# Second products with seven multiplications of eight: one fused DFT, gated MoE and MoE kernel on one core

## The chip, the cores and the metric

The kernel runs on one core of a Trainium2 chip. The metric is the device time of one execution in microseconds, the median of some runs. Every matmul in the main part is made in a 32-bit float format whose operands are rounded (F32R); to keep precision each operand is split in a high and a low part, and a product is three matmuls: high by high, high by low, low by high (`mm3`).

## The reference

```python
X = np.fft.fft(np.fft.fft(x, axis=1), axis=2).real           # x: (4, 3072, 256)
h = np.maximum(X @ w_in, 0.0)                                # (4, 3072, 1024)
u, v = h[..., :512], h[..., 512:]
v_n = (v - mean(v)) / np.sqrt(var(v) + 1e-06)
v_s = np.einsum('ts,bsd->btd', w_spatial, v_n) + b_spatial[None, :, None]
y = (u * v_s) @ w_out                                        # w_out: 512 x 256
x2 = y.reshape(12288, 256)
gate = 1.0 / (1.0 + np.exp(-(x2 @ w_gate)))                  # 256 x 1536
out = (gate * (x2 @ w_val)) @ moe2_w_out                     # 1536 x 256
```

## The kernel before

The kernel has three parts. The first (to about 254 us) makes the transform, U and V, and stores both to DRAM. The second (254 to 1751 us), which the change touches, multiplies by w_spatial and then by w_out. The third (to the end) is the last MoE.

In the second part the product with w_spatial is done in two halves p of the batch, each by seven products of blocks instead of eight (Strassen's scheme). `leaves` lists them: (p, i, c), where i is one of the seven products in the order 3, 5, 1, 7, 4, 2, 6, and c one of three columns of 512 tokens. A leaf multiplies a V operand (3072/2 rows by 512) by a W operand (3072/2 by 512 tokens) into four PSUM banks, one for each 128 rows d of 512. The loop over leaves is divided in sixths, kp = 0 to 5. In each sixth TensorE does 2 x 4 products of three matmuls, each of 128x128 weights by 512 columns: 24 in a sixth, 144 in a leaf. Leaves take turns between banks 0 to 3 and 4 to 7.

The order of the instructions on each engine is the order of the program. In each sixth the loop writes, in this order:

- `evacuate(before, ..., kp, ...)` in the first four sixths: VectorE adds bank d of the leaf before to the sums in `C` (and so frees the bank). Where i is in `FINAL` (5, 4, 2 and 6), the sum is one block of v_s. It is multiplied by max(U, 0) to g (`scalar_tensor_tensor`), ScalarE casts g to its high part `gh`, and the low part `gl` is left for `finish_gate`, which the next sixth calls.
- `advance`: it loads operands two sixths ahead of their preparation (SP's queue) and prepares those that are needed three sixths later (LEAD). ScalarE scales V (`norm_job`), VectorE adds or subtracts two blocks where the scheme wants it (L929 for V, L933 for W), ScalarE casts to the high part (L942), and VectorE makes the low part (L950) one job later. W operands have a ring of four buffers, V operands one of seven, loads one of seven staging tiles. V operands for the next i are made in the leaves with c = 2, one in each sixth.
- `side_loads` in the fifth sixth: bias and the first two blocks of U, from SP's queue. `load_u` for the other two blocks stands behind the use of the first two, since U has two buffers.
- the 24 matmuls of the sixth.
- `second`, behind the fifth and the sixth sixth, where the leaf before is in `FINAL`: one half o of 128 output columns, 4 x 3 matmuls of 512 columns against `wo`, a copy of the bank by ScalarE, and with o = 1 the store of the 128x2x512 block to `x2_d` from ScalarE's queue.
- `background` in other leaves: the weights of the last MoE and w_out are made from 64-bit words, a step at a time; GpSimd makes sums of blocks for the third part.

There are 24 leaves in `FINAL`, and so 24 second products. The last two are woven into the end of this part and the beginning of the third.

Of the kernel before, what the change touches and what calls it, by code (L numbers as in the profile page):

```python
# [10 lines left out]
F32 = mybir.dt.float32  # L11
# [12 lines left out]
DM = 256  # L24
FF2 = 1536
P = 128
# [134 lines left out]
def layouts(x, moe_w_in, moe_w_spatial, moe_b_spatial, moe_w_out, moe2_w_gate, moe2_w_val, moe2_w_out):  # L161
# [18 lines left out]
    for at in (0, 32, 64):  # L180
# [6 lines left out]
    wg, wv = (w.reshape(2, P, 12, P) for w in (moe2_w_gate, moe2_w_val))  # L187
    arrays = {
# [6 lines left out]
        "w_out": moe_w_out.reshape(4, P, DM).transpose(1, 0, 2).reshape(P, 2, 512),  # L195
# [44 lines left out]
def tile_kernel(ctx: ExitStack, tc: tile.TileContext, t: dict, out: bass.AP):  # L240
# [5 lines left out]
    wg_d = [dram.tile([P, 896], F32, name=f"wg_d{i}") for i in range(12)]  # L246
    wv_d = [dram.tile([P, 1024], F32, name=f"wv_d{i}") for i in range(3)]
# [920 lines left out]
    wo = [gp.tile([P, 2, 512], F32R, tag=f"wo{n}", name=f"wo{n}") for n in "hl"]  # L1168
# [3 lines left out]
    taken, begun, stores = [], [], []  # L1172

    def background():
# [5 lines left out]
        elif begun:  # L1180
            first, kind, i = begun.pop()
            value, = from64_rest(first, new())
            if kind == "second":
                split(wo[0][:, i, :], wo[1][:, i, :], value)
            elif kind == "out":
                stores.append((wv_d[i // 2][:, i % 2 * 512 : i % 2 * 512 + 512], value))
            else:
# [11 lines left out]
                stores.append((wg_d[i][:, 0:384], value[:, 0:384]))  # L1199
                stores.append((wg_d[i][:, 384:896], sums))  # L1200
        else:
            for to, value in stores:
                nc.sync.dma_start(to, value)
            stores.clear()
# [6 lines left out]
    def evacuate(leaf, ps, d, side):  # L1211
# [41 lines left out]
    def finish_gate(side):  # L1253
        if "low" in side:
            side.pop("low")()

    def load_u(side, d):
        u = gp.tile([P, 512], F32, tag="u", name="u", bufs=2)
        nc.sync.dma_start(u, side["u_of"][:, d, :])
        side["u"].append(u)  # L1260

    def side_loads(leaf, side):
        p, i, c = leaf
        if i in (3, 4, 5):
            at = ((3 if i == 3 else 0) + c) * 512
            side["bias"] = gp.tile([P, 512], F32, tag="bias", name="bias")
            nc.sync.dma_start(side["bias"], t["bt"][:, at : at + 512].to_broadcast([P, 512]))
# [8 lines left out]
    def second(leaf, o, bank, side):  # L1276
# [355 lines left out]
```

## Time and profile before

| | |
|---|---|
| median of 3 runs | 2842.23 us (2842.18 to 2842.6) |
| the profiled execution | 2841.18 us, span 2839.1 us |
| TensorE, VectorE, ScalarE busy | 2827.8, 1998.9, 1416.4 us |
| GpSimd busy | 235.5 us |
| granted TensorE clock | 1.00 |

The span is from the first to the last instruction of the program; some 2 us of the execution lie outside it. A row of a group of instructions gives their number, busy time and mean duration. Instructions of one engine are pipelined, so that the next can start before one has ended; durations then add up to more than the busy time, and what an instruction costs its engine is the distance from start to start. A matmul of 512 columns lasts 0.39 us in the trace, while the next starts 0.23 us after it.

### The profile page before, as it was taken

How to read it: one execution, taken by the hardware profiler on the slowest of the kernel's cores; microseconds unless marked ns; L12 is line 12 of the kernel's file. 1: busy time of each engine (PE TensorE's matmuls, PEld its weight loads, DVE VectorE, ACT ScalarE, POOL GpSimd, SP SyncE). 2: the span in 40 equal slices, each digit the busy share in tenths (PEclk: the TensorE clock that was granted, in tenths of full speed). 3: DMA queues.
4: the chain of work that ended last, by engine and by line, in shares of the span. 5: the costliest groups of instructions: out<-in, count | busy, mean ns of one | idle time of the engine just before them, and what ended most of it. 6: DMA issues, size and time to landing. Idle time of an engine off the chain costs nothing.

```text
span 2839.1 us, 34286 instructions
## 1 busy us (share of the span) xinstructions
PE 2827.8 (100%) x12630; PEld 2360.2 (83%) x12630; DVE 1998.9 (70%) x2936; ACT 1416.4 (50%) x2264; POOL 235.5 (8%) x348
## 2 busy tenths in 40 slices
PE   9999999999999999999999999999999999999999
PEld 7998888888888888888888888888888888888887
DVE  8877757778847666677756666876667666766665
ACT  6886434334424424433424424665655565656565
POOL 5984000011000000000000000000000000000000
PEclk9999999999999999999999999999999999999999
DMA  8888757778847766677866683100000000000000
GB/s 300 292 314 324 274 198 260 266 261 299 275 143 261 257 227 238 213 268 262 284 207 213 214 285 108 61 23 30 30 30 1 30 30 30 23 8 30 30 15 15
DMA packets 150953, 470.89 MB, mean 166 GB/s; under 512 B 16769, under 2 KB 18689, under 8 KB 150401
## 3 DMA queue, kind: packets, MB, share of 16 engines
q1 hardware_dynamic: 144448, 440.52, 45.0%
q0 software_dynamic: 2448, 14.82, 1.4%
q10 hardware_dynamic: 3888, 13.37, 1.2%
q8 instruction: 98, 1.61, 0.2%
q14 instruction: 71, 0.57, 0.1%
HBM read 386.07 MB, written 82.58 MB: 165 GB/s over the span
## 4 chain that ended last, share of the span: by engine, by line
PE 96%; DVE 2%; DMA 1%; ACT 1%; issue 0%; SPq 0%; ACTq 0%; DVEq 0%
PE bank L261 30%; PE bank L262 30%; PE bank L263 30%; PE psv L262 1%; PE psv L263 1%; PE psv L261 1%; PE psu L261 1%; PE psu L262 1%; PE psu L263 1%; PE psf L261 1%; PE psf L262 1%; PE psf L263 1%; DMA st<-v_d 1%; PE psv L730 0%; PE psu L768 0%
## 5 line engine op out<-in xcount | busy, mean ns | idle before, releaser
L262 PE MATMUL bank<-wl,vh 128*128 128x512 f32 x2016 | 784.4, 389 | 0.2 <-DVE wl L950 0.2
L261 PE MATMUL bank<-wh,vh 128*128 128x512 f32 x2016 | 784.3, 389 | 0.0
L263 PE MATMUL bank<-wh,vl 128*128 128x512 f32 x2016 | 784.2, 389 | 0.0
L942 ACT CAST wh<-st 128x1024 fp32r<-128x1024 f32 x249 | 260.9, 1049 | 382.9 <-PE bank L263 231.0
L262 PEld LDWEIGHTS bank<-wl,vh 128*128 128x128 f32 x2016 | 378.4, 188 | 79.5 <-DVE wl L950 0.8
L261 PEld LDWEIGHTS bank<-wh,vh 128*128 128x128 f32 x2016 | 378.4, 188 | 78.5
L263 PEld LDWEIGHTS bank<-wh,vl 128*128 128x128 f32 x2016 | 378.4, 188 | 78.3
L950 DVE TENSOR_TENSOR wl<-st,wh 128x1024 fp32r<-128x1024 f32 x249 | 306.8, 1233 | 169.4 <-ACT wh L942 168.9
L261 PE MATMUL bank<-x,wgh 128*128 128x512 f32 x673 | 262.4, 390 | 0.5 <-ACT t L1511 0.4
L1497 DVE TENSOR_TENSOR t<-t,bank 128x512 f32<-128x512 f32 x144 | 98.9, 687 | 231.4 <-PE bank L263 231.4
L262 PE MATMUL bank<-x,wgh 128*128 128x512 f32 x673 | 261.8, 389 | 0.0
L263 PE MATMUL bank<-x,wgl 128*128 128x512 f32 x673 | 261.8, 389 | 0.0
L933 DVE TENSOR_TENSOR st<-st 128x1024 f32<-128x1024 f32 x177 | 217.7, 1230 | 50.5 <-DMA st<-in_wt 50.5
L1520 DVE TENSOR_TENSOR gl<-s,gh 128x512 fp32r<-128x512 f32 x288 | 199.4, 692 | 57.8 <-ACT gh L1518 44.4
L262 PE MATMUL bank<-gl,wv 128*128 128x512 f32 x576 | 224.1, 389 | 0.0
L261 PE MATMUL bank<-gh,wv 128*128 128x512 f32 x576 | 224.1, 389 | 0.0
L263 PE MATMUL bank<-gh,wv 128*128 128x512 f32 x576 | 224.1, 389 | 0.0
L916 ACT ACTIVATE st<-st,ln_all 128x512 f32<-128x512 f32 x162 | 123.3, 809 | 140.5 <-DMA st<-v_d 115.7
L1485 ACT ACTIVATE s<-s 128x512 f32<-128x512 f32 x144 | 91.0, 632 | 153.8 <-DVE s L1484 153.7
L261 PEld LDWEIGHTS bank<-x,wgh 128*128 128x128 f32 x673 | 126.3, 188 | 28.5 <-ACT s L1482 0.9
L263 PEld LDWEIGHTS bank<-x,wgl 128*128 128x128 f32 x673 | 126.3, 188 | 26.3
L262 PEld LDWEIGHTS bank<-x,wgh 128*128 128x128 f32 x673 | 126.3, 188 | 26.0
(267 smaller groups left out, 4490.4 us busy)
## 6 DMA issues: line engine op xcount, KB each, us to landing
st<-in_wt SPq DMA_DIRECT2D x424, 512.0 KB, 5.5
st<-v_d SPq DMA_DIRECT2D x140, 512.0 KB, 4.7
u_d<-tu SPq DMA_DIRECT2D x64, 384.0 KB, 5.4
u<-u_d SPq DMA_DIRECT2D x96, 256.0 KB, 5.7
v_d<-tv SPq DMA_DIRECT2D x92, 256.0 KB, 5.1
x_d<-x ACTq DMA_DIRECT2D x24, 512.0 KB, 4.9
raw<-x_d SPq DMA_DIRECT2D x24, 512.0 KB, 7.1
xt<-in_xh SPq DMA_DIRECT2D x23, 512.0 KB, 5.2
```

What stands on the lines that cost most here:

```text
L261: nc.tensor.matmul(out=ps, lhsT=w[0], rhs=x[0], start=first, stop=False, **kw)
L262: nc.tensor.matmul(out=ps, lhsT=w[0], rhs=x[1], start=False, stop=False, **kw)
L263: nc.tensor.matmul(out=ps, lhsT=w[1], rhs=x[0], start=False, stop=last, **kw)
L916: nc.scalar.activation(st[:, k, :], st[:, k, :], AF.Identity, scale=scale[:, at], bias=shift[:, at])
L933: nc.vector.tensor_tensor(out=tiles[0], in0=tiles[0], in1=tiles[1], op=op)
L942: nc.scalar.copy(hl[0], st)
L950: eng.tensor_tensor(out=hl[1], in0=st, in1=f(hl[0]), op=ALU.subtract)
L1485: nc.scalar.activation(s1, s1, AF.Sigmoid)
L1497: nc.vector.tensor_tensor(out=g["t2"], in0=g["t2"], in1=g["b"], op=ALU.add)
L1520: nc.vector.tensor_tensor(out=l, in0=s, in1=f(h), op=ALU.subtract)
```

## The change

22 of the 24 second products (all but the last two) get a scheme with seven products of eight as well. The 512 tokens are taken in two halves of 256 (`HC`), and for each pair of 128-row blocks d the product of a 2x2 arrangement (two outputs o, two blocks d, two halves of columns) is made of seven terms:

- `evacuate` keeps g of an even d, and with the odd d VectorE makes four differences of 256 columns (two tiles `ta`, `tb`). `take_piece` casts the pieces: 256 columns of the first g, all 512 of the second, both tiles. Low parts follow in `finish_gate`; the last piece (`late`) is cast in the fifth sixth. Pieces have one buffer each.
- `second` does terms, each of three matmuls of 256 columns, into four banks (those that the leaf before used): six terms of the first pair behind the third sixth, the seventh behind the fourth, all seven of the second pair behind the fifth.
- `combine` adds up the four banks: one copy by ScalarE and six additions by VectorE, written behind `advance` of the last sixth. `send` stores both halves from ScalarE's queue.
- The weights are laid out in blocks a11, a12, a22, a21 as the third part has them, and `background` adds the sums s1 to s4 and splits them; a21 goes to DRAM (`wa_d`) for the last two products.
- U and bias are asked for on GpSimd's queue instead of SP's. `load_u` now stands ahead of the casts. Stores left over from `background` are sent at the start of a leaf.
- The last two second products keep 24 matmuls of 512 columns, in another order for the last but one (`plain`: the first pair for both halves behind the first block of the last leaf). Pieces and `wo` lie in a pool `mp` of their own, which is closed behind the last second product and opened anew for the third part.

```diff
-        if "parts" in side:
-            gh, gl = (x[at] for x in side["parts"])
-        else:
-            gh = gp.tile([P, 512], F32R, tag="gh", name="gh", bufs=4)
-            gl = gp.tile([P, 512], F32R, tag="gl", name="gl", bufs=4)
-        nc.scalar.copy(gh, g)
-        finish_gate(side)
-        side["low"] = lambda: nc.vector.tensor_tensor(out=gl, in0=g, in1=f(gh), op=ALU.subtract)
-        side["g"].append((gh, gl))
         if d < 2:
             load_u(side, d + 2)
+        finish_gate(side)
+        if leaf not in SEVEN:
+            if "parts" in side or d < 3:
+                take_piece(side, "g", d, g)
+            else:
+                side["late"] = lambda: take_piece(side, "g", d, g)
+            return
+        if d % 2 == 0:
+            side["raw"] = g
+            if d == 0:
+                take_piece(side, 0, 0, g[:, 0:HC])
+            return
+        b1, b2 = side.pop("raw"), g
+        if d == 1:
+            take_piece(side, 0, 1, b2)
+        else:
+            take_piece(side, 1, 0, b1[:, 0:HC])
+            side["late"] = lambda: take_piece(side, 1, 1, b2)
+        ta, tb = (gp.tile([P, 512], F32, tag="cv", name="t", bufs=4) for _ in range(2))
+        for to, x, y in (
+            (ta[:, 0:HC], b1[:, HC:], b1[:, 0:HC]),
+            (tb[:, 0:HC], b2[:, HC:], b1[:, HC:]),
+            (ta[:, HC:], b2[:, HC:], ta[:, 0:HC]),
+            (tb[:, HC:], b2[:, 0:HC], ta[:, HC:]),
+        ):
+            tt(out=to, in0=x, in1=y, op=ALU.subtract)
+        take_piece(side, d // 2, 2, ta)
+        take_piece(side, d // 2, 3, tb)
+
+    HC = 256
+
+    def take_piece(side, pair, i, src):
+        n = src.shape[-1]
+        if "parts" in side:
+            hi, lo = (x[:, i, :] for x in side["parts"])
+        else:
+            k = (2, 1, 3, 2)[i] if pair == "g" else i
+            hi, lo = (mp.tile([P, n], F32R, tag=f"{x}{k}", name=f"b{x}") for x in "hl")
+        nc.scalar.copy(hi, src)
+        side["g"][pair, i] = (hi, lo)
+        side["lows"].append(lambda: nc.vector.tensor_tensor(out=lo, in0=src, in1=f(hi), op=ALU.subtract))
 
     def finish_gate(side):
-        if "low" in side:
-            side.pop("low")()
+        while side["lows"]:
+            side["lows"].pop(0)()
+
...
     def load_u(side, d):
         u = gp.tile([P, 512], F32, tag="u", name="u", bufs=2)
-        nc.sync.dma_start(u, side["u_of"][:, d, :])
+        nc.gpsimd.dma_start(u, side["u_of"][:, d, :])
         side["u"].append(u)
...
+    TERMS = {
+        1: ("a11", 0, 0, 0, 0),
+        6: ("s2", 2, 1, 0, 1),
+        5: ("s1", 2, 0, 1, 0),
+        7: ("s3", 3, 0, 1, 1),
+        3: ("s4", 1, 1, 2, 0),
+        4: ("a22", 3, 1, 2, 1),
+        2: ("a12", 1, 0, 3, 0),
+    }
+
+    SEVEN = {leaf for leaf in leaves[:-2] if leaf[1] in FINAL}
...
+    def second(side, pair, terms, bank):
+
+        for term in terms:
+            w, piece, half, acc, at = TERMS[term]
+            first = acc not in side["acc"]
+            if first:
+                side["acc"][acc] = banks(bank + acc)
+            w = slice(W_AT[w] * P, W_AT[w] * P + P)
+            mm3(
+                side["acc"][acc][:, at * HC : at * HC + HC],
+                [x[:, pair, w] for x in wo],
+                [x[:, half * HC : half * HC + HC] for x in side["g"][pair, piece]],
+                first,
+                pair == 1,
+                skip_group_check=True,
+            )
+
+    def combine(side, part, both, to):
+
+        x, y, z, w = (side["acc"][k] for k in range(4))
+        tt = nc.vector.tensor_tensor
+        p1, u2 = part[:, 0:HC], part[:, HC:]
+        nc.scalar.copy(p1, x[:, 0:HC])
+        tt(out=u2, in0=p1, in1=x[:, HC:], op=ALU.add)
+        tt(
+            out=both.rearrange("p (k n) -> p k n", k=2),
+            in0=u2.unsqueeze(1).to_broadcast([P, 2, HC]),
+            in1=y.rearrange("p (k n) -> p k n", k=2),
+            op=ALU.add,
+        )
+        tt(out=to[1][:, HC:], in0=both[:, HC:], in1=y[:, 0:HC], op=ALU.add)
+        tt(out=to[0][:, HC:], in0=both[:, 0:HC], in1=z[:, 0:HC], op=ALU.add)
+        tt(out=to[1][:, 0:HC], in0=both[:, HC:], in1=z[:, HC:], op=ALU.add)
+        tt(out=to[0][:, 0:HC], in0=p1, in1=w[:, 0:HC], op=ALU.add)
+        side["to"] = to
+
+    def combine_cv(side):
+        combine(side, *(lambda a: (a[0], a[1], a[2:]))([gp.tile([P, 512], F32, tag="cv", name="y", bufs=4) for _ in range(4)]))
+
+    def send(leaf, side):
         p, i, c = leaf
         mem, th = FINAL[i]
-        finish_gate(side)
-        ps = banks(bank)
-        for d in range(4):
-            at = (d % 2) * 256 + o * P
-            mm3(ps, [w[:, d // 2, at : at + P] for w in wo], side["g"][d], d == 0, d == 3)
-        if o == 0:
-            side["x2"] = gp.tile([P, 2, 512], F32, tag="x2", name="x2", bufs=1)
-        nc.scalar.copy(side["x2"][:, o, :], ps)
-        if o == 1:
-            nc.scalar.dma_start(x2_d[(2 * p + mem) * 6 + 3 * th + c], side["x2"])
+        for o in range(2):
+            nc.scalar.dma_start(x2_d[(2 * p + mem) * 6 + 3 * th + c][:, o, :], side["to"][o])
...
+        side = new_side()
+        final = before is not None and before[0][1] in FINAL
+        seven = before is not None and before[0] in SEVEN
         for kp in range(6):
-            if before is not None:
-                if kp < 4:
-                    evacuate(before[0], before[1][kp], kp, before[2])
-                else:
-                    finish_gate(before[2])
+            if kp == 0 and final:
+                send_stores()
+            if before is not None and kp < 4:
+                evacuate(before[0], before[1][kp], kp, before[2])
+            if final and kp == 4:
+                before[2].pop("late")()
+                finish_gate(before[2])
             advance(6 * n + kp + LEAD, 2)
+            if seven and kp == 5:
+                combine_cv(before[2])
             if kp == 4:
                 side_loads(leaf, side)
             wh, wl = ready["w", (p, i, c, kp)]
...
                         kp == 0 and k == 0,
                         kp == 5 and k == 1,
                     )
-            if before is not None:
-                if kp >= 4 and before[0][1] in FINAL:
-                    second(before[0], kp - 4, 4 - base + kp - 2, before[2])
+            if seven and kp in (2, 3, 4):
+                second(before[2], kp // 4, ((1, 6, 5, 7, 4, 3), (2,), (1, 6, 5, 7, 4, 3, 2))[kp - 2], 4 - base)
+            if final and kp == 5:
+                send(before[0], before[2])
```

## Rows read from the trace of the kernel before

**Rows 1.** The page's busy table: busy us (share of the span) xinstructions
```profile
PE 2827.8 (100%) x12630; PEld 2360.2 (83%) x12630; DVE 1998.9 (70%) x2936; ACT 1416.4 (50%) x2264; POOL 235.5 (8%) x348
```

**Rows 2.** The page's chain that ended last, shares of the span by engine
```profile
PE 96%; DVE 2%; DMA 1%; ACT 1%; issue 0%; SPq 0%; ACTq 0%; DVEq 0%
```

**Rows 3.** Windows: length, busy us of PE, PEld, DVE, ACT, POOL, clock, DMA share, GB/s
```profile
422.80:460.88 38.08, 38.08 (x170) 31.53 (x169) 31.63 (x38) 22.79 (x28) 0.00 (x0) 1.00 0.82 275
...
1173.51:1211.59 38.08, 38.08 (x169) 31.53 (x168) 30.23 (x37) 22.16 (x28) 0.00 (x0) 1.00 0.78 259
...
694.79:732.88 38.09, 38.09 (x170) 31.53 (x169) 30.77 (x39) 10.88 (x14) 2.21 (x4) 1.00 0.74 251
...
809.03:847.12 38.09, 38.09 (x170) 31.53 (x169) 16.91 (x23) 10.89 (x14) 0.00 (x0) 1.00 0.53 176
```

**Rows 4.** Timeline of TensorE, 512 columns, first and last of 55: start us, us, what
```profile
799.74 0.39 PE L262 MATMUL bank<-gl,woh 128*128 128x512 f32 x1
...
811.98 0.39 PE L262 MATMUL bank<-wl,vh 128*128 128x512 f32 x1
```

**Rows 5.** Timeline of TensorE, 384 columns, first and last of 19
```profile
119.81 0.33 PE L261 MATMUL psf<-c,fh 128*128 128x384 f32 x1
...
122.95 0.33 PE L263 MATMUL psf<-c,fl 128*128 128x384 f32 x1
```

**Rows 6.** Timeline of TensorE at 12 us, full 32-bit matmuls, eight merged
```profile
11.82 1.89 PE L503 MATMUL psx<-xt,ln_all 128*128 128x256 f32 x8
```

**Rows 7.** Timeline of weight loads behind a wait
```profile
40.80 0.19 PEld L261 LDWEIGHTS psv<-gh,ph 128*128 128x128 f32 x1 [0.36 <-ACT ph L453]
40.91 0.19 PEld L262 LDWEIGHTS psv<-gl,ph 128*128 128x128 f32 x1
```

**Rows 8.** Timeline of VectorE before and in the stretch at 422.80
```profile
418.24 0.69 DVE L1223 TENSOR_TENSOR g<-c,bank 128x512 f32<-128x512 f32 x1 [9.12 <-PE bank L263]
...
426.74 0.68 DVE L1223 TENSOR_TENSOR g<-c,bank 128x512 f32<-128x512 f32 x1
427.34 0.68 DVE L1224 TENSOR_TENSOR c<-bias,bank 128x512 f32<-128x512 f32 x1
...
430.28 1.41 DVE L929 SCALAR_TENSOR_TENSOR st<-st,ln_all 128x512 f32<-128x512 f32 x2
431.68 1.22 DVE L950 TENSOR_TENSOR wl<-st,wh 128x1024 fp32r<-128x1024 f32 x1
...
441.29 1.22 DVE L933 TENSOR_TENSOR st<-st 128x1024 f32<-128x1024 f32 x1
442.43 1.22 DVE L950 TENSOR_TENSOR vl<-st,vh 128x1024 fp32r<-128x1024 f32 x1
```

**Rows 9.** Timeline of TensorE: second half of a second product, next leaf's first matmul
```profile
420.07 0.39 PE L261 MATMUL bank<-gh,woh 128*128 128x512 f32 x1
...
422.80 0.39 PE L261 MATMUL bank<-wh,vh 128*128 128x512 f32 x1
```

**Rows 10.** Groups of VectorE instructions by shape: xcount | busy us, mean ns | idle before
```profile
L528 DVE TENSOR_TENSOR words<-et 128x256 f32<-128x256 f32 x2 | 0.8, 417 | 0.0
```

**Rows 11.** Waits from 422.80 to 460.88: us in total, times, longest
```profile
ACT st L916 <- DMA st<-v_d: 5.2, 2, 2.6
...
DVE st L929 <- ACT st L916: 2.9, 2, 2.4
```

**Rows 12.** Waits of SP's queue in the same stretch
```profile
SPq L882 <- DVE wl L950: 13.7, 6, 4.8
```

**Rows 13.** DMA issues by tile: xcount, KB each, median us to landing
```profile
u<-u_d SPq DMA_DIRECT2D x96, 256.0 KB, 5.7
...
st<-in_wt POOLq DMA_DIRECT2D x8, 512.0 KB, 7.9
```

More of the change, by code (lines that the diff above doesn't have):

```diff
@@ L1172, in tile_kernel, with send_stores @@
     taken, begun, stores = [], [], []
+    def send_stores():
+        for to, value in stores:
+            nc.sync.dma_start(to, value)
+        stores.clear()
     def background():
@@ L1182, in background @@
             value, = from64_rest(first, new())
-            if kind == "second":
-                split(wo[0][:, i, :], wo[1][:, i, :], value)
-            elif kind == "out":
+            if kind == "out":
                 stores.append((wv_d[i // 2][:, i % 2 * 512 : i % 2 * 512 + 512], value))
@@ L1198, in background @@
                     nc.gpsimd.tensor_tensor(out=s, in0=x, in1=y, op=op)
[L1199 to L1204 removed]
+                if kind == "second":
+                    for at, src in ((slice(0, 384), value[:, 0:384]), (slice(384, 896), sums)):
+                        split(wo[0][:, i, at], wo[1][:, i, at], src)
+                    parts = gp.tile([P, 512], F32R, tag="cv", name="parts", bufs=4)
+                    split(parts[:, 0:P], parts[:, P : 2 * P], value[:, 384:512])
+                    stores.append((wa_d[:, i * 256 : i * 256 + 256], f(parts[:, 0:256])))
+                else:
+                    stores.append((wg_d[i][:, 0:384], value[:, 0:384]))
+                    stores.append((wg_d[i][:, 384:896], sums))
+        else:
+            send_stores()
             if todo64:
@@ L1274, in side_loads, with plain @@
                 load_u(side, d)
-    def second(leaf, o, bank, side):
+    TERMS = {
[8 more added lines that the diff above has]
+    SEVEN = {leaf for leaf in leaves[:-2] if leaf[1] in FINAL}
+    def plain(side, pair, o, bank):
+        if pair == 0:
+            side["acc"][o] = banks(bank)
+        for d in (2 * pair, 2 * pair + 1):
+            if (o, d % 2) == (1, 0):
+                w = [a21[:, pair * 256 + k * P : pair * 256 + k * P + P] for k in range(2)]
+            else:
+                at = W_AT[f"a{o + 1}{d % 2 + 1}"] * P
+                w = [x[:, pair, at : at + P] for x in wo]
+            mm3(side["acc"][o], w, side["g"]["g", d], d == 0, d == 3)
@@ new lines, in plain_out @@
+    def plain_out(side, o, to=None):
+        to = gp.tile([P, 512], F32, tag="cv", name="y", bufs=4) if to is None else to
+        nc.scalar.copy(to, side["acc"][o])
+        side.setdefault("to", []).append(to)
+    def second(side, pair, terms, bank):
[13 more added lines that the diff above has]
+            )
@@ L1446, in tile_kernel @@
         if d == 0:
+            for o in range(2):
+                plain(before[2], 0, o, 4 - base + 2 + o)
+            before[2].pop("late")()
+            finish_gate(before[2])
             split_wg(0, staged_b[0])
@@ L1451, in tile_kernel @@
         if d == 1:
-            second(before[0], 0, 4 - base + 2, before[2])
+            plain(before[2], 1, 0, None)
+            plain_out(before[2], 0)
             split_wg(1, staged_b[2])
@@ L1460, in tile_kernel @@
         if d == 2:
-            second(before[0], 1, 4 - base + 3, before[2])
+            plain(before[2], 1, 1, None)
+            plain_out(before[2], 1)
+            send(before[0], before[2])
             for step in steps[2:6]:
                 step()
-    before = (leaf, ps, side)
     wst = A["w"].tile([P, 1024], F32, tag="wl", name="wst")
@@ L1578, in tile_kernel @@
             steps[7]()
-            second(leaf, 0, base, side)
-            second(leaf, 1, base + 1, side)
+            for o in range(2):
+                for pair in range(2):
+                    plain(side, pair, o, base + o)
+            mix.close()
+            mp = pool(ra, "mp", 1, "right")
+            last_x2 = mp.tile([P, 2, 512], F32, tag="x2", name="x2", bufs=1)
+            for o in range(2):
+                plain_out(side, o, last_x2[:, o, :])
+            send(leaf, side)
             for k in range(2):
```

31 lines of the change are left out of this document (20 added, 11 removed).

## Prediction, written before the changed kernel ran

> **What bounds the kernel now.** I read the page's busy table first. TensorE is busy for 2827.8 of 2839.1 us, VectorE for 1998.9, ScalarE for 1416.4 [rows 1]; the chain that ended last is TensorE for 96% [rows 2]. So time can only come from fewer TensorE cycles, and only while nothing else becomes late. The change touches 22 leaves, so I looked at their stretches next [rows 3]. A stretch runs from the first matmul of a leaf to the first of the next and holds the second product of the leaf before. Each is 38.08 us, and TensorE is busy for all 38.08, granted clock 1.00 (2.4 GHz): there is no wait in them to win. Beside that VectorE differs: 31.63 us in the stretch at 422.80, where the next V operands are made as well, 16.91 in the one at 809.03, 30.77 in the one at 694.79, which still works off what the stretch before it left. Three products go with each V (L261 to L263), so 144 matmuls belong to the leaf and 24 to the second product.
>
> **TensorE, part by part.** Matmuls of 512 columns start 12.24 us / 54 = 0.2267 us apart [rows 4], those of 384 columns 3.14 / 18 = 0.1744 [rows 5]. The old second product is 24 x 0.2267 = 5.44 us. The new one is 2 pairs x 7 terms x 3 = 42 matmuls of 256 columns, a shape that this trace has only in another number format. By the line through the two rows 256 columns take 0.1744 - 0.0523 = 0.122 us. [...] I take 0.122, as a load that starts with the matmul before it is 0.11 ahead and so is hidden. 42 x 0.122 = 5.12 us: 0.32 saved, x 22 = **7.0 us less** (bounds: 18.0 less, 41 more). One product of eight saves little, because halving the columns takes 0.227 only to 0.122. The new stretch without waits is 32.64 + 5.12 = 37.76 us.
>
> **VectorE, per leaf.** Its instructions start closer than they last: 512 columns 0.60 us apart (426.74, 427.34), 1024 columns 1.14 (441.29, 442.43), a V sum of two 1.40 (430.28, 431.68) [rows 8]. For 256 columns the trace shows 417 ns of duration [rows 10]; 0.60 less the difference in duration (0.683 - 0.417) gives 0.334 apart. Added: eight differences, 8 x 0.334 = 2.67; low parts of eight pieces, 6 x 0.60 + 2 x 0.334 = 4.27 in place of 4 x 0.60; the sums of accumulators, 5 x 0.334 + 0.60 = 2.27. Together 6.8 us more. In the stretch at 809.03 that is 23.7 of 37.76 and costs nothing; at 694.79 it is 37.6, just covered, where work can still be late by up to 1 us. At 422.80 it is 38.4: more than the stretch has.
>
> There are six such stretches, those of the third column of leaves 5, 4 and 2 in both halves (31.63 and 30.23 us stand for them in rows 3). I made a ledger of one. VectorE can begin when the last leaf's first accumulator is done. Now that is at 418.24, 4.56 us ahead of the stretch, because the second half of the second product still follows on TensorE; the leaf's own matmuls end at 420.07 [rows 8, 9]. With all products moved ahead of the last sixth nothing follows, and the lead shrinks to 420.07 - 418.24 = 1.83. VectorE must come through to the third sum of accumulators, since the next leaf's second accumulator is the bank which that sum frees; it is needed three matmuls, 0.68 us, into the next stretch. So it has 1.83 + 37.76 + 0.68 = 40.27 us. Its work till then: evacuation 4 x 3 x 0.60 = 7.20; low parts 4.27; differences 2.67; V 6 x (1.40 + 1.14) = 15.24; W six low parts and three sums, 9 x 1.14 = 10.26; first three sums 0.33 + 0.60 + 0.42 = 1.35. Sum 40.99: overdrawn by 0.7 us if it never waits.
>
> It does wait. In this stretch it now idles 6.2 us, 3.0 of them because it is ahead; that part goes. The other part is that a V sum stands behind ScalarE's scaling (2.9 us), itself behind the V load (5.2) [rows 11], which SP issues when a staging tile comes free, 13.7 us of waiting for VectorE's low parts [rows 12]: a later VectorE asks later. New is that the scaling stands behind casts of pieces that wait for the differences. I take 2.0 us of such waits, between 0 and 4. So each of the six stretches ends 2.7 us late (0.7 to 4.7): **6 x 2.7 = 16 us more** (4 to 28). The next stretch has slack enough to begin afresh.
>
> **The rest, at nothing.** ScalarE gets four more casts, two of them short, and one short copy for two long ones, some 1.3 us a leaf, where it is busy 22.8 of 38.1 at most [rows 3]. Its casts for the second pair wait for TensorE's first products, as the pieces have one buffer each; behind them stands the cast of a W operand that TensorE takes two sixths (10.9 us) later; if that cover went, TensorE would wait by as much as the cast is late. The two stores on ScalarE's queue wait for the last sum; behind them stand the next leaf's first casts, which are made after VectorE's evacuation anyway. U and bias go from SP's queue to GpSimd's. GpSimd is idle in the six stretches and busy for at most 2.21 us in the others [rows 3]; a load that it issued landed after a median 7.9 us against 5.7 for U by SP [rows 13], and U is used two sixths after it is asked for. On SP the operand loads no longer stand behind U, which may bring them forward a little; I count nothing. The split of moe_w_out into 14 blocks lies in stretches without second products. The last two leaves keep 24 matmuls of 512 columns; the copies of the last one wait for both halves (0 to 1 us).
>
> **Sum.** 2841.18 us is the time of the profiled execution (span 2839.1 and 2.1 around it); - 7.0 + 16.2 gives 2850.4. The median of the runs is 1.05 above that execution: **2851.4 us**. The forecast's own range, with 1.7 to 3.7 us per stretch, is 2845 to 2857; the ends of the bounds, 0.7 and 4.7, give 2839 and 2863.
>
> **Rivals.**
> VectorE keeps up (faster). Place: the third sum of accumulators in the six stretches. It decides from the point where work and waits to that sum stay under 40.3 us; then only the 7.0 us remain: 2835. For it: my 256-column spacing is worked out, not seen, and 15 such instructions at 0.28 would close the overdraft. Against it: every wait must vanish as well. Chance 0.14.
>
> Short matmuls at their floor. At 0.11 us, the distance of two loads, TensorE saves 0.82 x 22 = 18 us; the stretch shrinks to 37.26, and the overdraft grows by 0.5 to 3.2: 19 us in six. 2841.2: no change. Against it: both rows of this format lie 13 to 14 ns above columns / 2.4. Chance 0.15. The Trainium skill (TensorE: Matmul & The Clock Gate, "Back-to-back issue gap") puts a warm start-to-start distance at columns / 2.4 plus about 2.5 ns, an estimate of 109 ns here; at 512 columns it gives 216 where rows 4 have 227, so in this number format the trace does not agree.
>
> The V loads are late too, since staging tiles come free later: 4.7 us per stretch or more, 28 - 7 = 21 us more, 2863. For it: that wait is in rows 11 already. Chance 0.18.
>
> Weight loads bind the short matmuls, at the 384-column distance. 42 x 0.1744 = 7.32 us, 1.88 more per leaf, 41 us more; the longer stretch (39.96) gives VectorE time, some 3 us of waits remain: 2886. Against it: two loads 0.11 apart. Chance 0.06.
>
> **How the numbers follow.** Forecast 0.47, rivals 0.14, 0.15, 0.18, 0.06. The range reaches from the kept pace to beyond the late loads: 2834 to 2870; the load-bound case and tails stay out. A measurement here tells 0.2% (5.7 us) from no change. Faster by more than that: most of the first rival and a tail of the second, 0.17. Within: the rest of these and the forecast's low end, 0.27. Slower: 0.56.
>
> **What would show it.** Right: 42 matmuls of 256 columns about 0.122 us apart; stretches of 37.7 to 37.8 us in some 16 of the 22; six of 39 to 42, each ending with TensorE waiting for a sum of accumulators on VectorE, VectorE busy from edge to edge there. Wrong: all 22 alike (VectorE keeps up); starts 0.11 or 0.17 apart; waits in the middle of stretches, at the terms behind the third or fifth sixth; or GpSimd's loads named as what ended VectorE's waits.

## The result and the profile after

The changed kernel takes **2883.03 us** (2881.78 to 2885.18, 4 runs) against 2842.41 (2842.18 to 2842.88) for the kernel before: ratio 1.0143, 95% interval 1.0128 to 1.0158. It is slower, as forecast, but by 40.6 us where 9 were expected; the range ended at 2870. The profiled run took 2884.23 us, span 2882.5.

The busy table and the chain that ended last, in place of [rows 1, 2]:

```profile
PE 2837.2 (98%) x13026; PEld 2380.7 (83%) x13026; DVE 2156.4 (75%) x3336; ACT 1440.4 (50%) x2334; POOL 302.1 (10%) x471
...
PE 74%; DVE 11%; DMA 8%; ACT 3%; issue 3%; SPq 0%; POOL 0%; ACTq 0%; DVEq 0%; POOLq 0%
...
PE bank L263 23%; PE bank L264 22%; PE bank L265 22%; DMA st<-v_d 5%; DVE wl L952 2%; DVE st L935 2%; DMA st<-in_wt 1%; DMA words<-in_w_b 1%; ACT st L918 1%; DVE vl L952 1%; ACT wh L944 1%; DVE st L931 1%; PE psv L264 1%; PE psv L265 1%; PE psv L263 1%
```

TensorE had 96% of the chain and has 74%. VectorE has 11%, and the loads of V (st<-v_d) have 5%: two engines and a queue now pass the end on to each other. TensorE's busy time has even grown by 9.4 us, though its columns are fewer; what that is comes below.

Windows of the changed kernel (length, busy us of PE, PEld, DVE, ACT, POOL, clock, DMA share, GB/s), in place of [rows 3]: two of the six overdrawn stretches, one without V operands, and the stretches behind the first two.

```profile
423.68:464.71 41.03, 37.90 (x187) 31.87 (x185) 38.63 (x54) 23.48 (x31) 2.71 (x5) 1.00 0.80 262
464.71:504.84 40.13, 39.76 (x187) 33.25 (x187) 34.50 (x54) 10.95 (x15) 1.09 (x2) 0.96 0.66 223
825.38:863.12 37.74, 37.74 (x187) 32.06 (x186) 24.19 (x43) 12.13 (x17) 2.19 (x4) 1.00 0.40 125
...
1194.93:1239.33 44.40, 37.90 (x187) 31.88 (x186) 38.62 (x54) 23.36 (x31) 2.72 (x5) 0.98 0.75 251
1239.33:1279.78 40.45, 40.45 (x187) 33.85 (x188) 34.51 (x54) 10.94 (x15) 2.72 (x5) 0.93 0.71 243
```

The undisturbed stretch is 37.74 us (37.76 forecast). The overdrawn ones are 41.03 and 44.40, with VectorE busy for 38.6, and the stretches behind them are long too: in the last row TensorE is busy from edge to edge, at a granted clock of 0.93. What TensorE waited for in the second part of the changed kernel (us in total, times, longest):

```profile
PE bank L263 <- DVE y L1375: 24.4, 7, 6.5
PE bank L264 <- DVE bl L1295: 5.4, 2, 2.8
PE bank L263 <- DVE y L1382: 1.9, 5, 0.4
PE bank L264 <- DVE wl L952: 1.6, 2, 1.2
```

The first row is the wait that was forecast: a leaf's first matmul for the sums of accumulators, seven times, behind the six stretches and behind n = 13. The second, the low parts of the pieces in mid-stretch, was not. Before, the same question gives 0.2 us in all.

The distance from a leaf's first matmul to the next's (n counts the leaves from 0; before, all of these are 38.08, but n = 30, which is 33.21 and holds no second product), for the changed kernel and the main experiments told below:

| n | after | sums_first | sixteen_b | no_diffs | seven_free | nine_tiles | nine_first |
|---|---|---|---|---|---|---|---|
| 5 (of the six) | 41.04 | 37.74 | 38.08 | 40.09 | 43.33 | 39.93 | 37.74 |
| 6 | 40.12 | 38.66 | 37.74 | 39.81 | 40.69 | 40.01 | 37.74 |
| 13 | 39.38 | 41.60 | 37.92 | 37.74 | 39.04 | 37.74 | 37.74 |
| 14 (six) | 45.22 | 39.92 | 38.27 | 41.21 | 44.77 | 40.49 | 37.74 |
| 15 | 40.11 | 37.74 | 38.04 | 38.49 | 39.32 | 39.98 | 37.76 |
| 17 (six) | 43.17 | 37.74 | 38.08 | 40.59 | 43.70 | 39.92 | 37.74 |
| 18 | 39.76 | 39.56 | 37.99 | 40.80 | 40.30 | 38.54 | 37.74 |
| 26 (six) | 44.40 | 37.74 | 38.08 | 42.67 | 45.09 | 40.12 | 37.74 |
| 27 | 40.45 | 43.27 | 38.39 | 40.22 | 40.38 | 38.49 | 37.74 |
| 30 | 34.29 | 33.34 | 37.69 | 36.97 | 33.65 | 32.64 | 32.64 |
| 35 (six) | 43.82 | 41.99 | 38.08 | 45.23 | 41.89 | 40.49 | 37.74 |
| 36 | 38.51 | 37.74 | 39.64 | 38.51 | 40.68 | 39.97 | 37.76 |
| 38 (six) | 42.28 | 37.74 | 38.08 | 40.19 | 42.56 | 40.12 | 37.74 |
| 39 | 39.90 | 39.00 | 38.07 | 40.14 | 39.96 | 38.51 | 39.03 |

In the changed kernel the thirteen rows with a second product hold 47.5 us over 13 x 37.74 (16.2 forecast). The span's sum: 22 x 0.34 = 7.5 less, 47.5 more, 2.3 in n = 3, 30 and others, 1.0 behind the last stretch: 43.3, the measured difference of the spans (2882.5 - 2839.1 = 43.4).

### The profile page after: what moved, and what is told of

It reads as the page before. It is cut to its first block, busy times and chain, and to the rows that moved or that the text cites. A ratio compares the mean times of both kernels' runs of the same rounds, so it can differ in the third digit from the quotient of the medians.

```text
span 2882.5 us, 35764 instructions
## 1 busy us (share of the span) xinstructions
PE 2837.2 (98%) x13026; PEld 2380.7 (83%) x13026; DVE 2156.4 (75%) x3336; ACT 1440.4 (50%) x2334; POOL 302.1 (10%) x471
## 4 chain that ended last, share of the span: by engine, by line
PE 74%; DVE 11%; DMA 8%; ACT 3%; issue 3%; SPq 0%; POOL 0%; ACTq 0%; DVEq 0%; POOLq 0%
PE bank L263 23%; PE bank L264 22%; PE bank L265 22%; DMA st<-v_d 5%; DVE wl L952 2%; DVE st L935 2%; DMA st<-in_wt 1%; DMA words<-in_w_b 1%; ACT st L918 1%; DVE vl L952 1%; ACT wh L944 1%; DVE st L931 1%; PE psv L264 1%; PE psv L265 1%; PE psv L263 1%
## 5 line engine op out<-in xcount | busy, mean ns | idle before, releaser
L263 PE MATMUL bank<-wh,vh 128*128 128x512 f32 x2016 | 790.5, 392 | 26.3 <-DVE y L1375 24.4
L952 DVE TENSOR_TENSOR wl<-st,wh 128x1024 fp32r<-128x1024 f32 x249 | 306.0, 1231 | 53.4 <-ACT wh L944 53.0
L935 DVE TENSOR_TENSOR st<-st 128x1024 f32<-128x1024 f32 x177 | 217.8, 1231 | 46.5 <-DMA st<-in_wt 46.4
L1293 ACT CAST bh<-g 128x256 fp32r<-128x256 f32 (+1 forms) x92 | 47.6, 518 | 253.2 <-DVE g L1252 137.3
L263 PEld LDWEIGHTS bank<-x,wgh 128*128 128x128 f32 x673 | 126.3, 188 | 29.6 <-DVE s L1605 1.5
```

The lines of the kernel that those rows point to most:

```text
L263: nc.tensor.matmul(out=ps, lhsT=w[0], rhs=x[0], start=first, stop=False, **kw)
L935: nc.vector.tensor_tensor(out=tiles[0], in0=tiles[0], in1=tiles[1], op=op)
L952: eng.tensor_tensor(out=hl[1], in0=st, in1=f(hl[0]), op=ALU.subtract)
L1293: nc.scalar.copy(hi, src)
```

## The experiments

Two theories went in: **A**, the loss is VectorE's in the six stretches (its work, with the V loads that wait for it); **B**, it is the new queue for U and bias on GpSimd. In the runs on staging tiles and on the differences the two names stand for what is left of A, as each expectation says: the loads with their loop, or VectorE's work alone. Ratios are to the kernel before, run beside each.

**U and bias back on SP** (u_on_sp).

```diff
-        nc.gpsimd.dma_start(u, side["u_of"][:, d, :])
+        nc.sync.dma_start(u, side["u_of"][:, d, :])
...
-            nc.gpsimd.dma_start(side["bias"], t["bt"][:, at : at + 512].to_broadcast([P, 512]))
+            nc.sync.dma_start(side["bias"], t["bt"][:, at : at + 512].to_broadcast([P, 512]))
```

> One part undone: U and bias tiles are asked for on SP's queue again; all else as in the changed kernel. Theory A (VectorE is overdrawn in the six stretches in which V operands are made, and the next leaf's first matmul waits for its sums of accumulators; GpSimd's queue has no part in it): 2875 to 2895 us, the six waits in front of a leaf stay. Theory B (loads through GpSimd's queue make the V loads late, which landed after 5.7 us in the median instead of 4.7): at least half of the 41 us comes back, under 2863 us, and V loads land after 4.7 us again.

2880.03 us, ratio 1.0134 (1.0120 to 1.0148), an interval that overlaps the changed kernel's. V loads landed after a median 5.1 us (5.7 in the changed kernel, 4.7 before), and the time is what theory A said. The queue is not the cause.

**Sums ahead of the operand work** (sums_first).

```diff
+            if seven and kp == 5:
+                combine_cv(before[2])
             advance(6 * n + kp + LEAD, 2)
-            if seven and kp == 5:
-                combine_cv(before[2])
```

> One part moved: the sums of accumulators stand ahead of the operand work of the last sixth instead of behind it. Theory A (what holds TensorE at the leaf's edge is that the sums stand behind VectorE instructions that wait for V loads): the six waits at the edge, 23 us together, go to under 1 us each; what VectorE still owes shows up later, as waits of TensorE for low parts at the terms behind the third sixth of the next stretch, up to 4 us each: 2850 to 2872 us. Rival (VectorE blocks at the sums until the second pair's products are done, 32.3 us into each of 22 stretches, and loses that time for operands): 2885 us or more.

2856.73 us, 1.0050 (1.0036 to 1.0064). TensorE's waits, same view:

```profile
PE bank L264 <- DVE bl L1295: 12.7, 7, 3.7
PE bank L264 <- DVE wl L952: 0.4, 1, 0.4
```

All edge waits are gone, so the sums' place behind the last operands, on VectorE and with their copy on ScalarE, cost most of the loss (26.3 of 40.6 us). But the backlog is still there: it turns up half a stretch later, as low parts that are late for the terms behind the third sixth.

**Differences on GpSimd** (diffs_gpsimd).

```diff
-            tt(out=to, in0=x, in1=y, op=ALU.subtract)
+            nc.gpsimd.tensor_tensor(out=to, in0=x, in1=y, op=ALU.subtract)
```

> The four differences of a pair are made by GpSimd instead of VectorE (eight instructions of 256 columns a leaf). Theory A: VectorE's ledger in the six stretches falls by 2.7 us, below the time it has, so the waits at the leaf's edge shrink by 2 to 3 us each, to 1 to 3 us: 2855 to 2870 us. Rival (GpSimd's instruction of this size took 0.77 to 0.79 us, so four take 3.1 us and the low parts come late, in all 22 stretches): TensorE waits at the terms behind the third sixth in stretches that had no wait, 2883 us or more.

2917.84 us, 1.0273 (1.0257 to 1.0289): a miss. The groups by shape, of this kernel (xcount, then busy us, mean ns, idle before):

```profile
L1280 POOL TENSOR_TENSOR t<-g 128x256 f32<-128x256 f32 x88 | 115.7, 1324 | 174.6 <-DVE g L1252 95.0 <-DVE bl L1295 78.6 <-DMA x_d<-y 0.7
L1280 POOL TENSOR_TENSOR t<-g,t 128x256 f32<-128x256 f32 x88 | 77.4, 879 | 3.5
```

On VectorE, in the changed kernel:

```profile
L1280 DVE TENSOR_TENSOR t<-g,t 128x256 f32<-128x256 f32 x88 | 37.0, 421 | 1.5
L1280 DVE TENSOR_TENSOR t<-g 128x256 f32<-128x256 f32 x88 | 33.2, 416 | 0.8 <-DMA x_d<-y 0.8
```

The pieces came late (TensorE waited 23.8 us for low parts, 5.4 in the changed kernel), and ScalarE's scaling of V stood behind their casts (VectorE waited 83.0 us for it, 42.7 in the changed kernel). It says that GpSimd is no relief; it does not tell what VectorE's work costs.

**Seven products for 16 leaves only** (sixteen; the six stretches keep 24 matmuls, a21 is read from DRAM).

```diff
-    SEVEN = {leaf for leaf in leaves[:-2] if leaf[1] in FINAL}
+    SEVEN = {leaf for leaf in leaves[:-2] if leaf[1] in FINAL and (leaf[1] == 6 or leaf[2] != 1)}
...
+            if final and not seven and kp in (3, 4):
+                for o in range(2):
+                    plain(before[2], kp - 3, o, 4 - base + o, lowa)
```

> Seven products of eight in 16 of the 22 second products only; the six whose work falls in a stretch in which V operands are made and VectorE's ledger is overdrawn keep 24 matmuls of 512 columns (behind the fourth and fifth sixth), a21 being read from DRAM for them; U and bias stay on GpSimd's queue. Theory A: no wait at a leaf's edge is left, 16 x 0.34 us are saved: 2836 to 2840 us, faster than both kernels. Theory B (U on GpSimd's queue is what costs): over 2850 us still.

2861.60 us, 1.0062 (1.0049 to 1.0075): a miss of both theories, in part from how I placed it. Its copies of the banks stood on ScalarE behind the scaling of V: TensorE waited 5.9 us for them at four edges. It waited another 7.3 us elsewhere, 3.2 of them for W low parts, so the placing does not account for all of the miss.

**The same, with the six in their old arrangement, and the sums first** (sixteen_b; the main lines of the edit).

```diff
+            if final and not seven and kp >= 4:
+                for pair in range(2):
+                    plain(before[2], pair, kp - 4, 4 - base + kp - 2, lowa)
+                plain_out(before[2], kp - 4)
```

> Seven products only where the stretch has no V operands to add (16 leaves); the six others get the 24 matmuls, copies and low parts of the kernel before in their old places (behind the fifth and the sixth sixth), with a21 fetched from DRAM into a spare tile; and the sums of accumulators stand ahead of the operand work. Theory (the loss lies only in the six overdrawn stretches): all six return to 38.08 us, 16 stretches fall to 37.74, some 2 us of wait stay in the stretch that takes over a step of the background work (n = 13), 2842.7 - 16 x 0.34 + 2 = 2839 us, range 2836 to 2843. Rival (the seven products delay VectorE everywhere and the backlog is carried into the six): waits of 2 to 3 us each at three or more of the six, 2850 us or more.

2845.81 us (11 runs), 1.0009 (1.0000 to 1.0018): at most 0.2% slower than before, but above the 2843 at which the theory's range ended. The table shows the six back at 38.08 (n = 14 at 38.27), as expected, and no backlog. The 5.4 us of TensorE are spent elsewhere: n = 30 takes 4.5 us longer than before (a wait of 3.1 us for a W low part, then half clock), n = 36 has 1.9 over 37.74 (1.6 of it a copy of a bank). The loss was in the six, and the gain that remains is as small as such accidents. Two things were changed at once here: the sums first alone gave 2856.73, so leaving the six out is worth 11 us on top of that; what it is worth without the sums first, only the run before shows, with its own copies in the way.

**Filler matmuls** (filler).

```diff
-                        kp == 5 and k == 1,
+                        kp == 5 and k == 1 and not (d == 3 and n in (17, 26, 38)),
...
+            if kp == 5 and n in (17, 26, 38):
+                for m in range(8):
+                    dsl = slice(3 * P, 4 * P)
+                    mm3(ps[3], (vh[:, m % 2, dsl], vl[:, m % 2, dsl]), (wh[:, m % 2, :], wl[:, m % 2, :]), False, m == 7)
```

> The changed kernel with 24 needless matmuls of 512 columns (5.44 us of TensorE) added at the end of three of the six stretches (n = 17, 26, 38), which doubles part of one sum. There the next leaf waited 5.4, 6.7 and 4.5 us, with some 1.6, 2.2 and 1.3 us of half clock behind it. Theory (the fall of the clock is brought by TensorE standing idle): the added work takes the place of the idle time, no start-to-start of 0.42 us is left behind these three edges, and the time falls by the clock's share, 5.1 us, less 0.9 us where the wait was shorter than the filler: 2879 us, range 2875 to 2881. Rival (matmuls behind the edge are slow for another reason): the slow matmuls stay, and the time is 2883 to 2886 us.

2879.29 us (2874.82 to 2885.81), 1.0130 (1.0116 to 1.0144). The time alone decides nothing, its interval overlaps the changed kernel's. The trace, which is that of the slowest run (2885.81), does in part: behind the edges at n = 18 and 39 there is no row of starts 0.43 us apart, as there is in the changed kernel; at n = 27 a wait of 1.5 us remained, and behind it slow matmuls came again. Windows from these three edges on, columns as above:

```profile
907.24:912.00 4.76, 4.38 (x19) 3.36 (x19) 4.68 (x9) 0.41 (x1) 0.48 (x1) 1.00 0.90 309
1680.93:1686.00 5.07, 5.07 (x23) 3.96 (x22) 5.04 (x10) 0.82 (x2) 0.55 (x1) 1.00 0.68 234
1239.41:1245.00 5.59, 5.22 (x15) 3.86 (x16) 5.50 (x10) 0.79 (x2) 0.55 (x1) 0.69 0.85 292
```

**One more staging tile** (seven_tiles, the control, and eight_tiles). The control writes all low parts to one scratch tile and multiplies by high parts in their place; the space gives an eighth tile.

```diff
-            hi, lo = (mp.tile([P, n], F32R, tag=f"{x}{k}", name=f"b{x}") for x in "hl")
-        side["g"][pair, i] = (hi, lo)
+            hi = mp.tile([P, n], F32R, tag=f"h{k}", name="bh")
+            lo = mp.tile([P, 512], F32R, tag="ls", name="bl")[:, 0:n]
+        side["g"][pair, i] = (hi, lo if "parts" in side else hi)
...
+        if "s8" in state and state["count"] % 8 == 7:
+            state["count"] += 1
+            return state["s8"].tile(shape, dtype, tag="s8", name=name, bufs=1)
```

> Control for the next run: the changed kernel with all low parts of the pieces written to one scratch tile and the matmuls using the high part in their place (leaves the low-part terms of the second product out; every instruction and its size stay). VectorE does the same work, TensorE no longer waits for low parts in mid-stretch. Both theories: the edge waits behind the six stretches stay (about 25 us), the two mid-stretch waits (2.9 and 2.8 us) go or move to the next edge: 2872 to 2884 us.

> As the control, with the space so gained used for an eighth staging tile for operand loads (seven before), so that each V and W load can be asked for one load earlier. Theory A (the wait per stretch was mis-sized since V loads are late: VectorE's late release of a staging tile delays the next V load, whose landing delays VectorE again): VectorE's waits for ScalarE and the V loads in the six stretches fall from 4 to 5 us to under 1.5 us each and the edge waits to 0 to 2 us each: 2840 to 2858 us, at least 15 us under the control. Theory B (VectorE's added work alone, the loads being a symptom): within 4 us of the control.

2889.54 us for the control (1.0165, 1.0151 to 1.0179), 5.5 us above the expected range, which nothing here explains, and 2875.99 (1.0120, 1.0104 to 1.0135) with the tile: 13.6 us less, where A said 15 or more and B at most 4. So it is nearer to A, but misses A's time by 18 us. In the six stretches VectorE's waits for scaled V fell from 13.7 to 10.0 us in all (from 0.4 to 4.5 in each of the control's, and not the 4 to 5 that the expectation took for them).

**No differences** (no_diffs).

```diff
-        ta, tb = (gp.tile([P, 512], F32, tag="cv", name="t", bufs=4) for _ in range(2))
-        for to, x, y in (
-            (ta[:, 0:HC], b1[:, HC:], b1[:, 0:HC]),
-            (tb[:, 0:HC], b2[:, HC:], b1[:, HC:]),
-            (ta[:, HC:], b2[:, HC:], ta[:, 0:HC]),
-            (tb[:, HC:], b2[:, 0:HC], ta[:, HC:]),
-        ):
-            tt(out=to, in0=x, in1=y, op=ALU.subtract)
-        take_piece(side, d // 2, 2, ta)
-        take_piece(side, d // 2, 3, tb)
+        take_piece(side, d // 2, 2, b1)
+        take_piece(side, d // 2, 3, b2)
```

> The changed kernel without the four differences of each pair (the third and fourth piece are b1 and b2 themselves; leaves out that arithmetic): VectorE has 8 x 0.334 = 2.67 us less work in each leaf, all else stays. Changed kernel: edge waits of 3.8, 2.1, 2.9, 5.8, 7.0, 2.2 and 5.4 us behind the six stretches and behind stretch 13, two mid-stretch waits of 2.9 and 2.8, some 8 us of half clock. Theory A (the loop through the staging tiles carries a delay on, so that a us of VectorE's work costs more than a us): each edge falls by more than 2.7 us, most of them to under 1.5: 2842 to 2856 us. Theory B (one for one): six edges fall by 2.7 us or to nothing, some 15 us, and 4 us of the clock go: 2861 to 2867 us.

2872.97 us, 1.0108 (1.0093 to 1.0123). Both theories missed, to the same side: 6 x 2.67 = 16 us of VectorE's work gave back only 10. VectorE's wait for scaled V between 270 and 1700 us, in the kernel before and in the changed kernel (over this whole part it had not grown):

```profile
DVE st L929 <- ACT st L916: 45.5, 31, 2.6
...
DVE st L931 <- ACT st L918: 42.7, 31, 4.1
```

and in this one:

```profile
DVE st L931 <- ACT st L918: 52.5, 36, 4.2
```

Much of the time that VectorE saves it waits away again, for scaled V: 9.8 us more over this part, 7.9 of them in the six stretches (23.8 against 15.9).

**Two more staging tiles** (nine_tiles, and seven_free, its control). Pieces go to scratch, a block of weights is read in their place, low parts don't wait for a cast; two tiles of space come free.

```diff
+            hi, lo = (mp.tile([P, 512], F32R, tag=f"{x}s", name=f"b{x}")[:, 0:n] for x in "hl")
+        side["g"][pair, i] = (hi, lo) if "parts" in side else (wo[0][:, 0, 0:n], wo[0][:, 0, 0:n])
...
+        if "s8" in state and state["count"] % 9 >= 7:
+            state["count"] += 1
+            return state["s8"].tile(shape, dtype, tag="s8", name=name, bufs=2)
```

> The changed kernel with the pieces written to scratch and a block of weights read in their place (leaves the pieces out of the product; every cast, low part, difference and matmul stays in size and order, but no matmul waits for a piece and no cast for a matmul), and the space used for two more staging tiles, nine. Seven tiles gave 2889.5 us, eight 2876.0. Theory A (what is left at eight tiles is still mostly V loads): VectorE's waits for the scaling in the six stretches fall to under 1 us each, from 0.7 to 3.1, the edges to under 2 us each: 2845 to 2860 us. Theory B (what is left is VectorE's own work, with the clock): edges stay at 3 us and more at most of the six, 2866 to 2877 us.

> Control for the run with nine staging tiles (2857.6 us): the same kernel, pieces written to scratch and a block of weights read in their place, low parts made without waiting for a cast, but seven staging tiles as in the changed kernel. Theory A (nine tiles gained by the earlier V loads): VectorE's waits for the scaling return to 2 to 5 us in the six stretches, edges of 3 to 7 us, 2874 to 2890 us. Theory B (nine tiles gained since no matmul waits for a piece and no cast for a matmul): within 5 us of 2857.6.

2857.64 us with nine (1.0054, 1.0037 to 1.0071), 2887.86 with seven (1.0160, 1.0143 to 1.0177): A both times, though the edges with nine stayed at 2.2 to 2.8 us, over the 2 expected. Untying the pieces gave nothing; the two tiles gave 30 us. In the six stretches VectorE's waits for scaled V fell from 15.0 to 3.1 us; TensorE's slow matmuls, counted as told below, fell from 15.8 to 5.6 us as well. VectorE's and ScalarE's waits from 270 to 1700 us with seven:

```profile
DVE st L931 <- ACT st L918: 42.7, 29, 4.5
...
ACT st L918 <- DMA st<-v_d: 137.2, 45, 7.3
```

and with nine:

```profile
DVE st L935 <- ACT st L922: 13.1, 16, 3.1
...
ACT st L922 <- DMA st<-v_d: 50.7, 27, 5.5
```

**Nine tiles and the sums first** (nine_first; the two edits together).

> As the run with nine staging tiles (pieces left out of the product), and the sums of accumulators ahead of the last sixth's operand work. With nine tiles (2857.6 us) VectorE's waits for scaling were 0.5 us a stretch, and edges of 2.2 to 2.8 us, one or two 0.5 us behind them and 3.6 us of half clock were left. Theory A (what is left is VectorE's own work ahead of the sums, some 2.5 us a stretch; V's last operands, which the order now puts behind the sums, have slack in the next leaf): all edges go, all 22 stretches are 37.74, and the whole 7 us of TensorE show: 2834 to 2838 us. Theory B (VectorE's backlog returns as a wait for operands or sums within the next leaf, as low parts did with seven tiles): 2842 us or more.

2836.25 us, 0.9978 (0.9969 to 0.9988), beside 2842.03 for the kernel before. All but one of the rows with a second product fall to 37.74 or 37.76, and one wait is left in TensorE's list:

```profile
PE bank L263 <- DVE c L1251: 1.0, 1, 1.0
```

With both causes gone nearly the whole saving of TensorE shows (5.8 us of 7.5). But here no matmul waits for a piece either, and late low parts of pieces were the wait that the sums first alone had left (12.7 us). No run has the sums first and the pieces untied with seven tiles, so what the two tiles add to that is not shown. This kernel leaves the pieces out of the product, so it is no version to use; with the pieces in place there is no room for two more tiles. Of those that compute everything none beat the kernel before.

## Why the prediction was wrong, point by point

**TensorE's price was right.** Behind a third sixth, the changed kernel's first and last of 18 matmuls of 256 columns:

```profile
841.70 0.28 PE L263 MATMUL bank<-bh,woh 128*128 128x256 f32 x1
...
843.74 0.28 PE L265 MATMUL bank<-bh,wol 128*128 128x256 f32 x1
```

2.04 / 17 = 0.120 us apart, 0.122 forecast. The rivals with 0.11 and 0.1744 fall, and with them the bounds of 18.0 less and 41 more, which were worked out from these two distances ([rows 7], [rows 5]). The Trainium skill (TensorE: Matmul & The Clock Gate, "Back-to-back issue gap", which gives the formula for an isolated matmul) leads to an estimate of 109 ns; this trace does not agree with it. The time of the rival at 0.11 was added up wrongly: 2842.2 - 18 + 19 is 2843, not 2841.2, which is still no change.

**Place and cause were right.** Six stretches, VectorE busy nearly from edge to edge, the next leaf waiting for the sums of accumulators: that is the row of 24.4 us above. The rival in which VectorE keeps up falls. Nine of the 22 stretches took 37.74 us, where some 16 were expected, the six took 41.0 to 45.2, where 39 to 42 were, and one of the prediction's own signs of being wrong came true: waits in mid-stretch, at the terms behind the third sixth (5.4 us).

One of the seven edge waits, behind n = 13, has another cause, which the prediction did not have. There VectorE stands idle:

```profile
737.77 1.52 ACT L918 ACTIVATE st<-st,ln_all 128x512 f32<-128x512 f32 x2 [5.15 <-DMA st<-v_d]
739.20 0.35 ACT L1374 COPY y<-bank 128x256 f32<-128x256 f32 x1
739.58 0.42 DVE L1375 TENSOR_TENSOR y<-y,bank 128x256 f32<-128x256 f32 x1 [6.91 <-ACT y L1374]
```

`combine` begins with ScalarE's copy, and that copy stands in ScalarE's order behind the scaling of V, which waited for a V load. It starts 38.5 us into n = 13 and 36.0 into n = 34, the stretches ahead of n = 14 and 35; ahead of the other four of the six it starts 32.4 us in. So n = 14 and 35 began with part of these sums still to be made. The prediction counted this copy as a short one and did not ask what it stands behind.

**What failed is the size of the sum: 16.2 us of waits at six edges were forecast, 47.5 us were lost.** Of the 31 us between, some 10 are at the edges (26.3 us of waits). The other 21 are terms that the prediction put at nothing, and most of these are TensorE's own slow matmuls behind its waits.

At the edges the step that failed is "I take 2.0 us of such waits, between 0 and 4". The end of the stretch at 1194.93, which has the longest edge wait:

```profile
1236.01 1.45 DVE L931 SCALAR_TENSOR_TENSOR st<-st,ln_all 128x512 f32<-128x512 f32 x2 [2.41 <-ACT st L918]
1237.64 1.22 DVE L952 TENSOR_TENSOR wl<-st,wh 128x1024 fp32r<-128x1024 f32 x1 [0.18 <-ACT wh L944]
1238.86 0.42 DVE L1375 TENSOR_TENSOR y<-y,bank 128x256 f32<-128x256 f32 x1
1239.38 0.69 DVE L1376 TENSOR_TENSOR y<-y,bank 128x512 f32<-128x512 f32 x1
1240.10 0.42 DVE L1382 TENSOR_TENSOR y<-y,bank 128x256 f32<-128x256 f32 x1
```

The third sum ends at 1240.52, 7.1 us late by the ledger's own clock. And that stretch's waits:

```profile
ACT st L918 <- DMA st<-v_d: 9.6, 2, 5.4
...
DVE st L931 <- ACT st L918: 5.1, 3, 2.4
DVE wl L952 <- ACT wh L944: 0.6, 3, 0.2
```

5.7 us of the 7.1 are waits, and 1.4 are work that the ledger had at 0.7: the work term was short by 0.7, the wait term by 3.7. Over the six, such waits are 1.5 to 5.7 us, mean 3.2; in the stretch of which the ledger was made (n = 5) they are 2.3, near the 2.0. In the ledger a VectorE that runs late was to hide part of a wait that it had before (2.9 us, read from one stretch). But SP asks for a load only when VectorE gives a staging tile back, so lateness moves the load as well, and little of the wait goes: for scaled V alone VectorE waited 20.1 us in the six stretches before (2.4 to 4.7 in each) and 15.9 us after (1.1 to 5.1). SP's own waits in the stretch at 1194.93, which were 13.9 and 10.3 us in the same stretch before:

```profile
SPq L884 <- DVE wl L952: 24.2, 6, 10.4
SPq L884 <- DVE vl L952: 17.8, 5, 4.6
```

The runs with eight and nine tiles, against controls with seven, show this loop by itself; no_diffs shows its other face, that faster work is in part waited away. The rival "the V loads are late too" named this cause at 0.18 and priced it at 4.7 us a stretch, 2863. The nine tiles bear its cause out; its price took 4.0 us of waits where the mean is 3.2, and it too counted nothing behind the edges.

**Terms that were missing.** First, TensorE's clock: the changed kernel behind the edge at n = 6.

```profile
464.71 0.50 PE L263 MATMUL bank<-wh,vh 128*128 128x512 f32 x1 [3.14 <-DVE y L1375]
465.05 0.40 PE L264 MATMUL bank<-wl,vh 128*128 128x512 f32 x1
...
467.04 0.63 PE L263 MATMUL bank<-wh,vh 128*128 128x512 f32 x1
467.47 0.63 PE L264 MATMUL bank<-wl,vh 128*128 128x512 f32 x1
467.89 0.63 PE L265 MATMUL bank<-wh,vl 128*128 128x512 f32 x1
...
470.23 0.40 PE L265 MATMUL bank<-wh,vl 128*128 128x512 f32 x1
470.46 0.40 PE L263 MATMUL bank<-wh,vh 128*128 128x512 f32 x1
```

After a wait of 3.1 us starts are 0.43 us apart from 466.62 to 469.60, then 0.23 again. In the second part 91 matmuls start over 20 ns late with no idle time ahead of them (one in the trace of before); together that is 13.7 us, and most of why TensorE's busy time grew though its columns are fewer. Second, a backlog lives on past an edge. "The next stretch has slack enough to begin afresh" holds for VectorE in the stretches behind the six, none of which ends with a wait for the first sum. It does not hold for TensorE: with its slow matmuls these six stretches took 12.4 us over 37.74. And n = 14 and 35 of the six themselves began late, as told above; their low parts were late in mid-stretch (2.8 and 2.6 us). So 16.2 us forecast against 47.5: 26.3 of edge waits (24.4 + 1.9), 5.4 for low parts, some 13.3 of slow matmuls, and 2.3 that the restarts cost.

**At nothing, and nothing:** on GpSimd's queue U landed after a median 4.1 us (5.7 on SP before) and bias after 6.2 (5.6), and they cost no time that u_on_sp could show. The two last leaves cost at most the 1.0 us behind the last stretch, the end of the range given.

## What to carry to other kernels

An engine that frees the buffers of its own inputs hides little of its input waits by being late (15.9 of 20.1 us stayed here): count such waits in full, in each of the stretches that they decide, and ask how many buffers the loop has. A change that saves 0.3 us on the bounding engine and adds 6.8 to one that is 83% busy in some stretches is decided in those stretches. Sums that free the next stage's banks belong ahead of work that is due later, on each engine that has a part in them. And each us of waiting on TensorE may cost more than a us: here 31.7 us of waits came with 15.6 us of slow matmuls and restarts.

## What the hardware showed that was not expected

TensorE's clock after idle time. Windows of the changed kernel (columns as above), first around the edge at n = 6, and then behind the one at n = 27:

```profile
464.71:466.30 1.59, 1.22 (x4) 0.76 (x5) 1.50 (x4) 0.00 (x0) 0.00 (x0) 1.00 0.64 126
466.30:469.60 3.30, 3.30 (x9) 2.54 (x9) 3.30 (x6) 0.41 (x1) 0.55 (x1) 0.54 1.01 399
469.60:474.60 5.00, 5.00 (x23) 4.11 (x22) 4.97 (x11) 2.14 (x3) 0.55 (x1) 0.97 0.71 228
...
1239.33:1240.30 0.97, 0.97 (x2) 0.83 (x3) 0.89 (x2) 0.00 (x0) 0.00 (x0) 0.50 0.87 224
1240.30:1245.30 5.00, 5.00 (x14) 3.70 (x13) 5.00 (x9) 1.17 (x2) 0.55 (x1) 0.55 0.91 310
```

The granted clock is 0.50 to 0.55, that is 1.2 in place of 2.4 GHz, once beginning 1.6 us after the restart, once with it, after waits of 3.1 and 6.5 us. Behind the wait of 1.5 us at 1558.83 the clock stayed at 1.00:

```profile
1558.83:1565.00 6.17, 5.80 (x24) 4.53 (x25) 6.02 (x11) 1.36 (x2) 0.55 (x1) 1.00 0.64 207
```

That idle time brings the fall is what filler's two clean edges speak for; its third edge, half clock behind 1.5 us, and this one, full clock behind as much, leave open what decides in between.

GpSimd's 256-column differences at 1324 and 879 ns, against about 420 on VectorE, were the other surprise. Beside them VectorE's own long instructions grew a little, 1231 to 1279 ns for L952 (mean over 249).
